# Streaming the moving operand's columns in other orders, in seven of twelve groups of a feed-forward block

## The chip, the cores and the metric

The kernel runs on one core of a Trainium2 chip. The metric is the device time of one execution in microseconds (us). Three runs of the kernel before gave 462.64, 462.67 and 462.92 us; the median is 462.67 us. The execution that the profiler recorded took 462.61 us.

The engines are named as the profile names them: PE is TensorE's matmuls, PEld its weight loads, DVE is VectorE, ACT is ScalarE, POOL is GpSimd, SP is SyncE with its DMA queue. A matmul here has a stationary operand (loaded first, 128 columns) and a moving operand, whose columns are streamed through; its output has one column for each column of the moving operand and lies in PSUM, where further matmuls add to it.

## The reference

Two stages follow each other. The first is a gated recurrence over 768 time steps for 4 batches and 8 heads of 40 channels; its outcome is a matrix x of 3072 tokens by 320 channels. The second is a feed-forward block on x:

```
h = x @ w_in                                       # 320 -> 2048
g = np.maximum(h, 0.0) + alpha * np.minimum(h, 0.0)
return (g @ w_out).astype(np.float32)              # 2048 -> 320
```

All of it is float32. The change touches the two matrix products of the second stage alone.

## The kernel before

The 3072 tokens are taken in 12 groups of 256 (`g` from 0 to 11), each of two chunks of 128. The recurrence is computed chunk by chunk as attention-like products, and the feed-forward of earlier groups is laid between those. The order of all work is written by hand: a list of named steps for the start (`ORDER`, line 638) and a pattern that repeats for each group (`PATTERN`, line 655). Each engine runs its instructions in that order.

Float32 accuracy is had by splitting each operand into a high part and a low part of type fp32r (`WH`, `WL`, `XH`, `XL`, `OH`, `OL`, `gh`, `gl`) and adding the products high by high, high by low and low by high.

The feed-forward of one group has 8 pairs of 128 hidden channels (`fp` from 0 to 7).

- Up (`up_steps`, line 703): for each of the two halves `e` of a pair, eight matmuls (lines 713 to 720) add to 256 columns of the PSUM tile `ph`. The stationary operand is a 128x128 block of the input weights, the moving operand is x by channel, one column for each of the group's 256 tokens. That is 16 matmuls for a pair and 128 for a group. ACT then takes the negative part (line 723), DVE adds the two slopes (line 728), ACT and POOL split the outcome into `gh` and `gl` (lines 737 and 739).
- Down (`down`, line 743; the matmul is line 750): the stationary operand is a 128x128 block of `gh` or `gl`, the moving operand is a row block of the output weights, `OH` or `OL`, of 320 columns. For each half `e` and each chunk `j` there are three matmuls, which add to `po[j]`. That is 12 for a pair and 96 for a group. The two PSUM tiles `po` have one buffer each: the next group's first down matmul needs the last copy out of them.
- Finish (`finish`, line 778): DVE copies the two `po` to `ob` in SBUF (line 783), and one DMA writes the group's 256 rows of the output (line 784).

Every matmul has its own weight load, which runs while the matmul before it streams.

Of the kernel before, what the change touches and what calls it, by code (L numbers as in the profile page):

```python
# [17 lines left out]
def kernel(ctx: ExitStack, tc: tile.TileContext, q, k, v, i_gate, f_gate, o_gate, w_in, w_out, alpha, out):  # L18
    nc = tc.nc
    B, H, S, D = q.shape  # L20
    DM, DFF = w_in.shape
    P = 128
# [30 lines left out]
    WH, WL = [None, None], [None, None]  # L53
# [5 lines left out]
    W2 = const.tile([P, DFF], F32R, tag="W2", name="W2")  # L59

    NB = 4
# [562 lines left out]
        yield  # L624

    NP = NF // 2
    LAG = 2
    LEAD = 4
    OFF = 0
# [6 lines left out]
    OBA = range(0)  # L636
# [54 lines left out]
    class FeedForward:  # L691
# [11 lines left out]
        def up_steps(self, split=True):  # L703
            g, fp = self.g, self.named
            self.named += 1
            XH, XL, X2, X2L = self.x
            ph = ps_h.tile([P, 2, GT], F32, tag="h", name=f"ph{g}_{fp}")
            for e in range(2):
                fs = slice((2 * fp + e) * P, (2 * fp + e + 1) * P)
                half, f0 = divmod((2 * fp + e) * P, DH)  # L710
                hs = slice(f0, f0 + P)
                dst = ph[:, e]
                nc.tensor.matmul(dst, WH[half][:, 0, hs], XH[:, 0], start=True, stop=False)  # L713
                nc.tensor.matmul(dst, WH[half][:, 1, hs], XH[:, 1], start=False, stop=False)  # L714
                nc.tensor.matmul(dst, WL[half][:, 0, hs], XH[:, 0], start=False, stop=False)  # L715
                nc.tensor.matmul(dst, WL[half][:, 1, hs], XH[:, 1], start=False, stop=False)  # L716
                nc.tensor.matmul(dst, W2[:, fs], X2, start=False, stop=False)  # L717
                nc.tensor.matmul(dst, WH[half][:, 0, hs], XL[:, 0], start=False, stop=False)  # L718
                nc.tensor.matmul(dst, WH[half][:, 1, hs], XL[:, 1], start=False, stop=False)  # L719
                nc.tensor.matmul(dst, W2[:, fs], X2L, start=False, stop=True)  # L720
            yield
            gt = late_pool.tile([P, 2, GT], F32, tag="g", name=f"g{g}_{fp}", bufs=3)
            nc.scalar.activation(gt, ph, AF.Relu, scale=-1.0)  # L723
            yield
            y = ph if split else gt
            for e in range(2):
                f = 2 * fp + e
                nc.vector.scalar_tensor_tensor(  # L728
                    out=y[:, e], in0=gt[:, e], scalar=oma[:, f : f + 1], in1=ph[:, e], op0=ALU.mult, op1=ALU.add
                )  # L730
            yield
            if g == 1 and fp < BEHIND:
                both = sb.tile([P, 2, 2, GT], F32R, tag=f"sp{fp % 2}", name=f"gg{g}_{fp}", bufs=1)
                gh, gl = both[:, 0], both[:, 1]
            else:
                gh, gl = (late_pool.tile([P, 2, GT], F32R, tag=f"g{x}", name=f"g{x}{g}_{fp}", bufs=3) for x in "hl")
            nc.scalar.copy(gh, y)  # L737
            yield
            (nc.vector if split else nc.gpsimd).tensor_tensor(gl, y, gh.bitcast(F32), ALU.subtract)  # L739
            self.done.append((gh, gl))  # L740
            yield

        def down(self, fp):
            if fp == 0 and self.g != 1:
                self.po = [ps_o.tile([P, DM], F32, tag=f"o{j}", name=f"po{self.g}_{j}") for j in range(GC)]
            po, (gh, gl) = self.po, self.done[fp]

            def add(e, j, x, W, **ends):
                f = 2 * fp + e
                nc.tensor.matmul(po[j], x[:, e, j * P : (j + 1) * P], W[f // NB][:, f % NB], **ends)  # L750

            def high(e, j):
                add(e, j, gh, OH, start=fp + e == 0, stop=False)
                add(e, j, gh, OL, start=False, stop=False)

            def low(e, j):
                add(e, j, gl, OH, start=False, stop=2 * fp + e == NF - 1)

            if self.g == NG - 1 and fp == NP - 1:

                for j in range(GC):
                    for step in (high, low):
                        for e in range(2):
                            step(e, j)
                    self.leave(j)
                return
            for step in (high, low):
                for e in range(2):
                    for j in range(GC):
                        step(e, j)  # L770
# [7 lines left out]
        def finish(self):  # L778
            g = self.g
            if g < NG - 1:  # L780
                ob = late_pool.tile([P, GC, DM], F32, tag="ob", name=f"ob{g}", bufs=1)
                for j in range(GC):
                    (nc.scalar.copy if g in OBA else nc.vector.tensor_copy)(ob[:, j], self.po[j])
                nc.sync.dma_start(out[g * GT : (g + 1) * GT, :].rearrange("(j p) e -> p j e", p=P), ob)
            if g == 1:
                turns[:] = ["b", "a"]
# [81 lines left out]
    def load_w_rest(i):  # L868

        pieces = []  # L870
        for e in range(2):
            cs = slice((i + e) * CW, (i + e + 1) * CW)
            rows, other = (slice(x * KR, (x + 1) * KR) for x in (e, 1 - e))
            pieces.append((rows, w_in[2 * P :, cs], W2[rows, cs], W2[other, cs]))
        return Weights(f"wr{i}", staging(f"wr{i}", ROOM[i][2]), pieces)

    def load_w_out(f):

        raw = sb.tile([P, 2, DM, 2], U32, tag="qS", name=f"wo{f}")
        src = w_out[f * P : (f + 2) * P, :].rearrange("(f p) c -> p f c", p=P)  # L880
        if src.dtype != F32:
            nc.sync.dma_start(
                raw.rearrange("p f c w -> p f (c w)"),
                w_out[f * P : (f + 2) * P, :].bitcast(U32).rearrange("(f p) c -> p f c", p=P),
            )
        to = slice(f % NB, f % NB + 2)

        def part(X):

            if X[f // NB] is None:  # L890
                out_block(f // NB)
            return lambda: X[f // NB][:, to]

        return Weights(f"wo{f}", raw, [(slice(0, P), src, lambda: part(OH)(), lambda: part(OL)())], False)
# [25 lines left out]
    def first_group():  # L920
# [333 lines left out]
        def block(name, make):  # L1254

            steps[name + "d"] = lambda: w.__setitem__(name, make())
            for op, do in dict(
                s=lambda: w[name].scale(), x=lambda: w[name].three(), y=lambda: w[name].shift(), j=lambda: w[name].join(),
                h=lambda: w[name].high(), H=lambda: w[name].high(1), l=lambda: w[name].low(), L=lambda: w[name].low(1),
                k=lambda: w[name].high(0, nc.gpsimd), K=lambda: w[name].high(1, nc.gpsimd),  # L1260
                p=lambda: w[name].low(0, nc.gpsimd), P=lambda: w[name].low(1, nc.gpsimd),
            ).items():
                steps[name + op] = do
# [4 lines left out]
        for i4 in (0, 2):  # L1268
            block(f"r{i4}", lambda i4=i4: load_w_rest(i4))
        for fp in range(NP):  # L1270
            block(f"o{fp}", lambda fp=fp: load_w_out(2 * fp))

        def named_ffn(g):
# [5 lines left out]
            steps[f"Z{g}"] = lambda: ffs[g].finish()  # L1279
            for fp in range(NP):  # L1280
                for tokens, split in (("URSGK", True), ("VrsgN", False)):
# [25 lines left out]
    start = len(nc.cur_bb.bb.instructions)  # L1307
# [34 lines left out]
```

## Time and profile before

| | |
|---|---|
| median of three runs | 462.67 us |
| the profiled execution, its own time | 462.61 us |
| its span (first to last instruction) | 460.9 us |
| PE busy | 454.9 us, 99% of the span |
| PEld busy | 444.1 us, 96% |
| DVE, ACT, POOL busy | 310.1, 314.0, 308.6 us |
| down matmuls in the program | 1152 of 320 columns |
| up matmuls in the program | 1536 of 256 columns |

Read it so: the engine that is busy all the time is PE, but a busy PE is not yet a PE at its peak, since matmuls are pipelined and their shown durations overlap. The time that one matmul takes of the span is the distance from its start to the start of the next one, not its shown duration (a down matmul is shown with some 308 ns, and the next one starts some 147 ns later). The rows below are mostly of that kind.

### The profile page before, as it was taken

How to read it: one execution, taken by the hardware profiler on the slowest of the kernel's cores; microseconds unless marked ns; L12 is line 12 of the kernel's file. 1: busy time of each engine (PE TensorE's matmuls, PEld its weight loads, DVE VectorE, ACT ScalarE, POOL GpSimd, SP SyncE). 2: the span in 40 equal slices, each digit the busy share in tenths (PEclk: the TensorE clock that was granted, in tenths of full speed). 3: DMA queues.
4: the chain of work that ended last, by engine and by line, in shares of the span. 5: the costliest groups of instructions: out<-in, count | busy, mean ns of one | idle time of the engine just before them, and what ended most of it. 6: DMA issues, size and time to landing. Idle time of an engine off the chain costs nothing.

```text
span 460.9 us, 11823 instructions
## 1 busy us (share of the span) xinstructions
PE 454.9 (99%) x4434; PEld 444.1 (96%) x4434; DVE 310.1 (67%) x659; ACT 314.0 (68%) x714; POOL 308.6 (67%) x398
## 2 busy tenths in 40 slices
PE   8999999999999999999999999999999999999997
PEld 6889999999999999999999999999999999999996
DVE  4789999667767766766676775776676675663321
ACT  4799898868858758758758659658758658423331
POOL 7735656756879679479779689479789687324231
PEclk9999999999999999999999999999999999999999
DMA  9997897749694673696793673598582341000000
GB/s 190 234 250 180 237 258 217 132 129 192 156 139 111 142 172 92 126 197 157 129 178 99 126 179 101 118 182 172 135 152 99 97 125 54 1 28 1 30 2 28
DMA packets 156163, 61.61 MB, mean 134 GB/s; under 512 B 140154, under 2 KB 145834, under 8 KB 156106
## 3 DMA queue, kind: packets, MB, share of 16 engines
q1 hardware_dynamic: 156026, 60.75, 58.8%
q8 instruction: 35, 0.57, 0.5%
q14 instruction: 22, 0.18, 0.2%
q10 hardware_dynamic: 80, 0.11, 0.1%
HBM read 36.90 MB, written 4.03 MB: 89 GB/s over the span
## 4 chain that ended last, share of the span: by engine, by line
PE 90%; DVE 4%; ACT 2%; SPq 2%; DMA 1%; issue 1%; DVEq 0%; ACTq 0%
PE po L750 36%; PE ph L713 5%; PE ph L716 5%; PE ph L718 5%; PE ph L715 5%; PE ph L714 5%; PE ph L717 5%; PE ph L720 5%; PE ph L719 5%; PE pH L376 4%; PE pS L477 4%; PE pH L337 1%; PE p L566 1%; PE pu L181 1%; PE pI L401 1%; PE pS L1071 1%
## 5 line engine op out<-in xcount | busy, mean ns | idle before, releaser
L739 POOL TENSOR_TENSOR gl<-g,gh 128x512 fp32r<-128x512 f32 x74 | 95.9, 1297 | 37.2 <-ACT gh L737 30.5
L750 PE MATMUL po<-OH,gh 128*128 128x320 f32 x368 | 110.2, 310 | 0.0
L750 PE MATMUL po<-OL,gh 128*128 128x320 f32 x368 | 109.4, 308 | 0.0
L723 ACT ACTIVATE g<-ph 128x512 f32<-128x512 f32 x96 | 57.5, 599 | 68.1 <-PE ph L720 62.6
L728 DVE SCALAR_TENSOR_TENSOR g<-g,oma,ph 128x256 f32<-128x256 f32 x148 | 63.5, 471 | 36.7 <-ACT g L723 36.7
L750 PEld LDWEIGHTS po<-OL,gh 128*128 128x128 f32 x368 | 69.2, 188 | 0.0
L750 PE MATMUL po<-OH,gl 128*128 128x320 f32 x368 | 69.0, 308 | 0.1
L750 PEld LDWEIGHTS po<-OH,gh 128*128 128x128 f32 x368 | 69.0, 187 | 0.0
L750 PEld LDWEIGHTS po<-OH,gl 128*128 128x128 f32 x368 | 57.7, 187 | 0.3 <-DVE gl L739 0.3
L713 PE MATMUL ph<-XH,WH 128*128 128x256 f32 x192 | 57.4, 299 | 0.5 <-DVE g L728 0.5
L716 PE MATMUL ph<-XH,WL 128*128 128x256 f32 x192 | 53.5, 279 | 0.0
L715 PE MATMUL ph<-XH,WL 128*128 128x256 f32 x192 | 53.4, 278 | 0.0
L714 PE MATMUL ph<-XH,WH 128*128 128x256 f32 x192 | 53.4, 278 | 0.0
L717 PE MATMUL ph<-X,W 128*128 128x256 f32 x192 | 53.3, 278 | 0.0
L718 PE MATMUL ph<-XL,WH 128*128 128x256 f32 x192 | 53.3, 278 | 0.0
L720 PE MATMUL ph<-X2L,W 128*128 128x256 f32 x192 | 53.3, 277 | 0.0
L719 PE MATMUL ph<-XL,WH 128*128 128x256 f32 x192 | 53.2, 277 | 0.0
L363 ACT CAST E<-pS 128x512 bf16<-128x512 f32 x72 | 41.1, 581 | 15.1 <-DVE pS L360 14.5
L448 ACT ACTIVATE E<-Lb,gates 128x128 f32<-128x128 f32 x160 | 50.1, 393 | 0.0
L737 ACT CAST gh<-g 128x512 fp32r<-128x512 f32 x74 | 44.7, 617 | 7.4 <-DVE g L728 5.0
L360 DVE TENSOR_TENSOR pS<-pS,E 128x512 f32<-128x512 f32 x36 | 24.9, 695 | 31.4 <-PE pS L477 28.9
L451 POOL TENSOR_SCALAR_AFFINE_SELECT E<-E 128x512 f32<-128x512 f32 x40 | 26.8, 670 | 20.0 <-ACT E L448 19.9
(196 smaller groups left out, 1138.3 us busy)
## 6 DMA issues: line engine op xcount, KB each, us to landing
Lb<-L_d SPq DMA_DIRECT2D x20, 512.0 KB
wo<-in_moe_w_out_dram SPq DMA_DIRECT2D x8, 640.0 KB
wi<-in_moe_w_in_dram SPq DMA_DIRECT2D x8, 512.0 KB
qn<-in_q_dram SPq DMA_DIRECT2D x24, 160.0 KB
kn<-in_k_dram SPq DMA_DIRECT2D x24, 160.0 KB
og<-in_o_gate_dram SPq DMA_DIRECT2D x24, 160.0 KB
va<-in_v_dram SPq DMA_DIRECT2D x24, 160.0 KB
out_dram<-ob SPq DMA_DIRECT2D x11, 320.0 KB
```

Source lines behind the costliest of these rows:

```text
L713: nc.tensor.matmul(dst, WH[half][:, 0, hs], XH[:, 0], start=True, stop=False)
L714: nc.tensor.matmul(dst, WH[half][:, 1, hs], XH[:, 1], start=False, stop=False)
L715: nc.tensor.matmul(dst, WL[half][:, 0, hs], XH[:, 0], start=False, stop=False)
L716: nc.tensor.matmul(dst, WL[half][:, 1, hs], XH[:, 1], start=False, stop=False)
L717: nc.tensor.matmul(dst, W2[:, fs], X2, start=False, stop=False)
L718: nc.tensor.matmul(dst, WH[half][:, 0, hs], XL[:, 0], start=False, stop=False)
L719: nc.tensor.matmul(dst, WH[half][:, 1, hs], XL[:, 1], start=False, stop=False)
L720: nc.tensor.matmul(dst, W2[:, fs], X2L, start=False, stop=True)
L723: nc.scalar.activation(gt, ph, AF.Relu, scale=-1.0)
L728: nc.vector.scalar_tensor_tensor(out=y[:, e], in0=gt[:, e], scalar=oma[:, f : f + 1], in1=ph[:, e], op0=ALU.mult, op1=ALU.add)
L739: (nc.vector if split else nc.gpsimd).tensor_tensor(gl, y, gh.bitcast(F32), ALU.subtract)
L750: nc.tensor.matmul(po[j], x[:, e, j * P : (j + 1) * P], W[f // NB][:, f % NB], **ends)
```

## The change

A row of 320 columns is 20 lines of 16 columns (64 bytes each), one of 256 columns is 16 lines. Two small functions rearrange an operand: `lines(x, a)` makes a view in which first every a-th line is taken, beginning with line 0, then every a-th line beginning with line 1, and so on. With a = 10 on 20 lines the order is 0, 10, 1, 11, 2, 12 and so on; with a = 4 it is 0, 4, 8, 12, 16, 1, 5 and so on. `in_order` cuts a row into the same pieces but leaves it in sequence.

- Down, groups 3 to 6, with a = 10, 4, 5 and 2: the moving operand (`OH`, `OL`) is streamed in the new order. `po` is written without gaps, so its columns stand in the order of the stream. The copy in `finish` puts them back: it reads `po` in sequence and writes `ob` line by line to their places.
- Up, groups 7 to 9, with a = 8, 4 and 2: the moving operand (x) and the output `ph` are both rearranged, so each sum lands in its place at once, and nothing behind it changes.
- In the other groups the value is None, and operands and outputs are as before. The up matmuls' eight lines became a loop with the same order of matmuls.

```diff
+    D_LINES = {3: 10, 4: 4, 5: 5, 6: 2}
+    U_LINES = {7: 8, 8: 4, 9: 2}
+
+    def lines(x, a):
+        return x if a is None else x.rearrange("p (h l c) -> p l h c", l=a, c=16)
+
+    def in_order(x, a):
+        return x if a is None else x.rearrange("p (l h c) -> p l h c", l=a, c=16)
...
-                nc.tensor.matmul(dst, W2[:, fs], X2L, start=False, stop=True)
+                pairs = [(W[half][:, kt, hs], X[:, kt]) for W, X in ((WH, XH), (WL, XH), (WH, XL)) for kt in range(2)]
+                pairs = pairs[:4] + [(W2[:, fs], X2)] + pairs[4:] + [(W2[:, fs], X2L)]
+                for i, (W, X) in enumerate(pairs):
+                    nc.tensor.matmul(
+                        lines(dst, U_LINES.get(g)), W, lines(X, U_LINES.get(g)), start=i == 0, stop=i == 7
+                    )
...
-                nc.tensor.matmul(po[j], x[:, e, j * P : (j + 1) * P], W[f // NB][:, f % NB], **ends)
+                row = lines(W[f // NB][:, f % NB], D_LINES.get(self.g))
+                nc.tensor.matmul(po[j], x[:, e, j * P : (j + 1) * P], row, **ends)
...
-                    (nc.scalar.copy if g in OBA else nc.vector.tensor_copy)(ob[:, j], self.po[j])
+                    nc.vector.tensor_copy(lines(ob[:, j], D_LINES.get(g)), in_order(self.po[j], D_LINES.get(g)))
```

No instruction moves on any engine: matmuls, copies and DMAs stand in the same order in both programs, at the same addresses. What differs in the rows are the shapes, and a few waits. On PE, where group 4's down matmuls begin (`po4` is that group's sums, `gh4_0` its first pair's high part), there stood before:

```order
L376 MATMUL pH11_1_3195<-vb11_2654,E3_11_2953 128x42
L750 MATMUL po4_0_3208<-OH0_104,gh4_0_3081 128x320
L750 MATMUL po4_0_3208<-OL0_105,gh4_0_3081 128x320
L750 MATMUL po4_1_3209<-OH0_104,gh4_0_3081 128x320
L750 MATMUL po4_1_3209<-OL0_105,gh4_0_3081 128x320
```

and now:

```order
L376 MATMUL pH11_1_3195<-vb11_2654,E3_11_2953 128x42
L758 MATMUL po4_0_3208<-OH0_104,gh4_0_3081 128x320 [waits PE_49]
L758 MATMUL po4_0_3208<-OL0_105,gh4_0_3081 128x320
L758 MATMUL po4_1_3209<-OH0_104,gh4_0_3081 128x320 [waits PE_49]
L758 MATMUL po4_1_3209<-OL0_105,gh4_0_3081 128x320
```

Two matmuls got a wait on PE's own semaphore, for the count that group 3's last down matmuls reach; the same is found at the start of groups 5, 6 and 7. In exchange, PE has 143 instructions that only wait, where it had 153.

On PE, the first half of group 7's first up block (`ph7_0`) was

```order
L713 MATMUL ph7_0_4775<-XH7_4650,WH0_102 128x256
L714 MATMUL ph7_0_4775<-XH7_4650,WH0_102 128x256
L715 MATMUL ph7_0_4775<-XH7_4650,WL0_103 128x256
L716 MATMUL ph7_0_4775<-XH7_4650,WL0_103 128x256
L717 MATMUL ph7_0_4775<-X27_4652,W2_76 128x256
L718 MATMUL ph7_0_4775<-XL7_4651,WH0_102 128x256
L719 MATMUL ph7_0_4775<-XL7_4651,WH0_102 128x256
L720 MATMUL ph7_0_4775<-X2L7_4653,W2_76 128x256
```

and is now

```order
L725 MATMUL ph7_0_4775<-XH7_4650,WH0_102 128x8x2x16 x2
L725 MATMUL ph7_0_4775<-XH7_4650,WL0_103 128x8x2x16 x2
L725 MATMUL ph7_0_4775<-X27_4652,W2_76 128x8x2x16
L725 MATMUL ph7_0_4775<-XL7_4651,WH0_102 128x8x2x16 x2
L725 MATMUL ph7_0_4775<-X2L7_4653,W2_76 128x8x2x16
```

The eight matmuls are the same ones in the same order, and only the shape of the output (and of the moving operand) differs.

## Rows read from the trace of the kernel before

**Rows 1.** The page's first part: busy time, share of the span and instructions of each engine; and from its second part the granted TensorE clock in 40 slices of the span, in tenths of full speed.

```profile
PE 454.9 (99%) x4434; PEld 444.1 (96%) x4434; DVE 310.1 (67%) x659; ACT 314.0 (68%) x714; POOL 308.6 (67%) x398
...
PEclk9999999999999999999999999999999999999999
```

**Rows 2.** Busy time of each engine in four stretches of the span; the columns are the stretch, its length, busy us and instructions of each engine, granted clock, DMA share and GB/s. Groups 3 to 9 have their changed work in the third.

```profile
0.00:20.00 20.00, 18.09 (x138) 14.19 (x139) 11.05 (x22) 12.65 (x32) 15.05 (x35) 1.00 0.96 196
20.00:113.00 93.00, 92.13 (x838) 89.05 (x837) 78.31 (x156) 79.51 (x174) 53.30 (x63) 1.00 0.85 206
113.00:393.00 280.00, 280.00 (x2927) 276.53 (x2924) 193.40 (x421) 200.02 (x470) 220.54 (x283) 1.00 0.62 134
393.00:461.00 68.00, 64.64 (x543) 64.30 (x540) 27.30 (x62) 21.84 (x40) 19.73 (x18) 1.00 0.04 16
```

**Rows 3.** What PE waited for, over the whole span: us in total, times, longest.

```profile
PE warm L154 <- POOL ident masks.py:199: 1.4, 1, 1.4
PE ph L713 <- DVE g L728: 0.5, 1, 0.5
PE pg L1161 <- DVE gates L979: 0.5, 1, 0.5
PE pb L1030 <- DVE E L1075: 0.3, 1, 0.3
```

**Rows 4.** The chain that ended last, its part from 148 to 393 us: shares by line.

```profile
by line: PE po L750 40.4%; PE ph L713 6.3%; PE pH L376 5.5%; PE ph L716 5.3%; PE ph L715 5.3%; PE ph L714 5.3%; PE ph L717 5.3%; PE ph L720 5.2%; PE ph L718 5.2%; PE ph L719 5.2%; PE pS L477 5.2%; PE pI L401 2.2%; PE p L566 1.9%; PE pu L181
```

**Rows 5.** The same chain's longest pieces of down matmuls: start us, us, what, and how many.

```profile
177.10 5.27 PE po L750 x36
...
212.23 5.27 PE po L750 x36
...
247.02 5.28 PE po L750 x36
...
281.92 5.28 PE po L750 x36
```

**Rows 6.** PE in order of time, an up block and a down block behind it: start us, us shown, line, operation, tiles, shape.

```profile
205.08 0.28 PE L713 MATMUL ph<-XH,WH 128*128 128x256 f32 x1
205.19 0.28 PE L714 MATMUL ph<-XH,WH 128*128 128x256 f32 x1
...
205.87 0.28 PE L720 MATMUL ph<-X2L,W 128*128 128x256 f32 x1
205.99 0.31 PE L750 MATMUL po<-OH,gh 128*128 128x320 f32 x1
```

**Rows 7.** The same view, another up block of the same shape (16 matmuls, of which the second and the last are shown, and what follows).

```profile
183.77 0.28 PE L714 MATMUL ph<-XH,WH 128*128 128x256 f32 x1
...
185.42 0.28 PE L720 MATMUL ph<-X2L,W 128*128 128x256 f32 x1
185.54 0.73 PE L477 MATMUL pS<-qS,kS 120*128 120x128 bf16 x10
```

**Rows 8.** The same view, two places near the start: a bf16 matmul whose moving operand is 128 columns read four times over (line 94), with the start of the next matmul; and six fp32 matmuls of 128 columns, each with its own fp32 weight load (line 566).

```profile
24.56 0.38 PE L94 MATMUL pb<-later,ident 128*128 128x512 bf16 x1
24.78 0.39 PE L1030 MATMUL pb<-LP,pick 96*128 96x128 bf16 x4
...
209.58 0.82 PE L566 MATMUL p<-ident,xn 128*128 128x128 f32 x6
```

**Rows 9.** The copies of a group's sums: all 14 between 148 and 393 us (duration min/median/max ns, first and last start), and who waited for them; then group 3's two, and PE where group 4's down matmuls begin.

```profile
L783 DVE COPY ob<-po x14: 480/486/492, 158.9 to 368.9; 128x320 f32<-128x320 f32 x14
...
who waited for it (us, times):
...
L783 DVE COPY ob<-po x2: 480/486/492, 193.7 to 194.2; 128x320 f32<-128x320 f32 x2
...
196.89 0.39 PE L750 MATMUL po<-OH,gh 128*128 128x320 f32 x1
```

**Rows 10.** PE waited for by others, between 148 and 393 us, at the up matmuls' tile: us in total, times.

```profile
who waited for it (us, times):
  ACT g L723: 32.0, 28
```

More of the change, by code (lines that the diff above doesn't have):

```diff
@@ L712, in up_steps @@
                 dst = ph[:, e]
[L713 to L719, printed above, removed]
-                nc.tensor.matmul(dst, W2[:, fs], X2L, start=False, stop=True)
+                pairs = [(W[half][:, kt, hs], X[:, kt]) for W, X in ((WH, XH), (WL, XH), (WH, XL)) for kt in range(2)]
[4 more added lines that the diff above has]
+                    )
             yield
```

## The prediction

> **What bounds the kernel now.** I read the busy shares first. [...] The stretches say where that holds without a gap: from 113 to 393 us PE is busy for 280.00 of 280.00 us [rows 2], and that stretch holds nearly all of the changed work. Third, what PE waited for: four waits, 2.7 us together, none on a copy or a transfer of the groups that change [rows 3]. Last the chain that ended last: between 148 and 393 us the down matmuls (line 750) have 40.4% of it, the eight up lines 5.2 to 6.3% each [rows 4]. So the reader is to see one thing: in the changed groups each nanosecond more or less between two matmul starts is a nanosecond of the span. Nothing else of the change lies on that path.
>
> **What one matmul takes.** A down matmul: 36 in a row take 5.27 or 5.28 us of the chain, 146.5 ns each [rows 5]. An up matmul: in one block starts go from 205.08 to 205.99 us over eight, 114 ns each (113.3 over longer stretches) [rows 6]; in another block, same shape, same clock, 15 steps from 183.77 to 185.54 us are 118 ns each [rows 7]. So up matmuls have two speeds. The mean over both: lines 714 to 720 have 5.2 to 5.3% of 245 us for 112 matmuls each, 114 to 116 ns [rows 4]; I take 115.
>
> **The change part by part.** Down, groups 3 to 6: 4 x 96 = 384 matmuls, 384 x 146.5 ns = 56.3 us of the span. Up, groups 7 to 9: 3 x 128 = 384 matmuls, 384 x 115 ns = 44.2 us. Neither their number, nor their columns, nor their order or addresses change; only the order of the 16-column lines within one stream does. A down matmul has 20 runs of 16 columns where it had one of 320, an up matmul 16 where it had one of 256: 384 x 20 + 384 x 16 = 13,824 runs.
>
> What a run costs, the trace of before does not show for fp32r. The nearest row is the bf16 matmul that reads 128 columns four times over, so that its stream jumps back three times: it takes 0.22 us for 512 columns, 0.43 ns a column, where the clock allows 0.417 [rows 8]. Its jumps cost at most some 3 ns each, and within the rounding nothing. But bf16 has half the bytes of fp32r in a column, so this row does not exclude a cost at full width. Bounds, then.
>
> Above: one TensorE cycle lost at each run. [...]
>
> [...] 320 columns at one per cycle are 133 ns, and a down matmul takes 146.5; if an order removed all of the difference, 384 x 13 ns = 5.1 us would go. [...]
>
> I take zero between -7.4 and +5.8. The down spacing is the same 146.5 ns in each long row of 36 [rows 5], although these rows take different weight blocks and have other engines and DMAs beside them; a cost that depended on which addresses meet would rather vary. And the jump row lies near zero.
>
> The copies: group 3 to 6 have two each, eight in all, 486 ns now [rows 9]; their output is now written in runs of 16 columns. Nobody waits for them. Group 3's end at 194.2 + 0.49 = 194.7 us, and PE first writes the tile again at 196.89 [rows 9]. Even at double the duration they would end at 195.7. DVE is busy for 193 of 280 us [rows 2], so 8 x 0.49 us more are no load. Zero.
>
> The waits: eight first down matmuls (two in each of groups 4 to 7) wait for PE's own count of the group before. That count is reached before the copy starts, at 193.7 us, and the waiting matmul starts at 196.89 [rows 9], 3 us later. Queued behind it would be all of PE, but it is met on arrival: zero. The ten instructions fewer that only waited stood beside streaming matmuls; zero too.
>
> The sum: 462.61 us of the profiled execution (460.9 us of span and 1.7 around it) + 0. The median of the runs is 462.67, 0.06 above, and I predict **462.7 us**.
>
> [...] The new up outputs are not contiguous, in pieces of 64 bytes. [...]
>
> **The rivals.**
>
> [...]
>
> *Faster: the extra 13 ns of a down matmul come from two reads that meet.* While 320 columns stream, the next 128 weight columns are read too; if both come to the same part of the memory from time to time, the order decides how often. For it: the extra itself, and the two speeds of up blocks that are alike in everything but the moment at which they start [rows 6, 7]: something falls into step or does not. Against it: the constancy over addresses. Some orders would then gain and some lose. If two of the four down orders reach 133 ns, 2 x 96 x 13 = 2.5 us go, and with the up groups always at 113.3, another 384 x 1.7 ns = 0.65: 459.5 us. [...]
> [...]
>
> *Slower: outputs written in pieces.* If the up output in pieces goes in at half speed, an up matmul takes 2 x 107 = 213 ns instead of 115, and 384 x 98 ns = 38 us are added: 500 us. ACT, which waits for the up matmuls 28 times already [rows 10], would only wait more. [...]
>
> That the change does nothing at all to the stream, because the hardware walks the same lines at the same pace, is the forecast itself.
>
> **How the numbers follow.** What the measurement can tell from no change is about 0.2%, 0.9 us, so "same" is 461.7 to 463.6. No measurable change 0.44; each run costs 0.24; outputs in pieces 0.06; faster 0.26. That gives faster 0.26, same 0.44, slower 0.30. The range: 457.5 leaves out the lower part of the faster case (some 0.05); 470 leaves out the pieces (0.06) and runs that cost over 1.3 cycles (some 0.08). The likeliest case's own range is 461.7 to 463.6.
>
> **What would show it.** Right: in groups 3 to 6, rows of 36 down matmuls at 5.27 us, in groups 7 to 9 up starts 113 to 118 ns apart, PE without waits, copies of any duration that nobody waits for. Wrong: a spacing in one changed group that differs from its unchanged neighbours (groups 2, 10, 11), and by how much for each value of a. A cost per run would be the same for a = 10, 4, 5 and 2, since all have 20 runs; a meeting of reads would differ between them. A wait of PE on itself at the start of groups 4 to 7, or a first matmul there later than after the copy, would say that the waits cost something after all.

## The result, and the profile after

The kernel with the change takes 466.21 us (median of three runs, 466.12 to 467.0) where the one before took 462.67: a ratio of 1.008, with a 95% interval of 1.0057 to 1.0103. It is slower by 3.5 us, 0.8%. The execution that the profiler recorded took 466.12 us, its span is 464.4 us, and 3.5 us more than before stand in both.

The page after, to be read beside [rows 1]: busy time of each engine, granted clock.

```profile
PE 458.2 (99%) x4434; PEld 447.4 (96%) x4434; DVE 311.2 (67%) x659; ACT 314.1 (68%) x714; POOL 308.3 (66%) x398
...
PEclk9999999999999999999999999999999999999999
```

PE has grown by 3.3 us at the same number of instructions and the same clock. DVE grew by 1.1, but not in the rearranged copies, which last as long as before (below); ACT and POOL stand still. So PE did not wait longer: it worked longer. The stretches say the same, answering to the last two of [rows 2] (stretch, its length, busy us and instructions of each engine, clock, DMA share, GB/s; the border is set 4 us later, where the program has come about as far).

```profile
113.00:397.00 284.00, 284.00 (x2940) 280.43 (x2938) 194.55 (x422) 200.18 (x471) 220.25 (x283) 1.00 0.61 132
397.00:465.00 68.00, 64.16 (x534) 63.82 (x532) 26.97 (x61) 21.84 (x40) 19.74 (x18) 1.00 0.04 16
```

PE is busy for 284.00 of 284.00 us. What PE waited for (us in total, times, longest; answers to [rows 3]):

```profile
PE warm L154 <- POOL ident masks.py:199: 1.4, 1, 1.4
PE pg L1169 <- DVE gates L987: 0.7, 1, 0.7
PE ph L725 <- DVE g L735: 0.5, 1, 0.5
PE pb L1038 <- DVE E L1083: 0.3, 1, 0.3
```

There is no new wait, and no row of PE waiting for itself or for a copy. So the 3.5 us lie in the distances between matmul starts, and the next view has them: PE at the tile `po` in groups 2 to 7, one group a row (stretch, length, busy us of these 96 matmuls, clock, DMA share, GB/s).

```profile
127.10:159.30 32.20, 14.95 (x96) 1.00 0.68 134
162.20:194.60 32.40, 15.41 (x96) 1.00 0.64 130
197.50:229.50 32.00, 15.17 (x96) 1.00 0.84 163
232.50:264.80 32.30, 14.98 (x96) 1.00 0.63 134
267.70:300.40 32.70, 15.47 (x96) 1.00 0.55 129
303.40:335.80 32.40, 14.97 (x96) 1.00 0.84 163
```

The first and the last row are groups left as they were. Between them stand a = 10, 4, 5 and 2: +0.46, +0.22, +0.03 and +0.52 us, 1.2 us in sum. The same for the up matmuls at the tile `ph`, groups 6 to 10; groups 7 to 9 have a = 8, 4 and 2:

```profile
254.30:283.20 28.90, 16.31 (x128) 1.00 0.66 150
289.70:319.20 29.50, 16.86 (x128) 1.00 0.83 156
325.20:354.60 29.40, 16.79 (x128) 1.00 0.65 147
360.90:390.20 29.30, 17.04 (x128) 1.00 0.38 108
396.60:423.70 27.10, 16.30 (x128) 1.00 0.04 13
```

Beside the two unchanged groups that is some +0.6, +0.5 and +0.7 us. A busy time counts overlapping matmuls once, so it is only near the distance of starts; start to start over all matmuls of the trace, the up matmuls take 2.3 us more than before (2.0 of them in groups 7 to 9, and 0.2 in group 1, which is unchanged), the down matmuls 1.3, and all others together none.

The chain shows the distance itself, in the pieces of 36 down matmuls that answer to [rows 5]: start us, us, what, how many.

```profile
177.52 5.44 PE po L758 x36
...
212.96 5.37 PE po L758 x36
...
247.90 5.28 PE po L758 x36
...
283.13 5.41 PE po L758 x36
...
319.17 5.28 PE po L758 x36
```

Divided by 36: 151.1 ns in group 3, 149.2 in 4, 146.7 in 5, 150.3 in 6, and 146.7 in group 7, which is as before. From here on a spacing is the mean distance from a matmul's start to the next one's, within the blocks of one group; the few first steps of a block that are 80 to 110 ns longer than the rest are left out. In the whole trace it is 146.5 in unchanged down groups and 151.2, 148.8, 146.8 and 151.7 for a = 10, 4, 5 and 2; in unchanged up groups 114 to 116.5, and 120.0, 119.8 and 121.4 for a = 8, 4 and 2.

The copies, answering to [rows 9]:

```profile
L791 DVE COPY ob<-po x14: 480/486/492, 159.1 to 371.8; 128x320 f32<-128x320 f32 x14
...
who waited for it (us, times):
```

To write the columns back in pieces of 16 costs a copy nothing, and still nobody waits for it.

### The profile page after: what moved, and what is told of

It is laid out like the page before. It is cut to its first block, busy times and chain, and to the rows that moved or that the text cites. A ratio compares the mean times of both kernels' runs of the same rounds, so it can differ in the third digit from the quotient of the medians.

```text
span 464.4 us, 11813 instructions
## 1 busy us (share of the span) xinstructions
PE 458.2 (99%) x4434; PEld 447.4 (96%) x4434; DVE 311.2 (67%) x659; ACT 314.1 (68%) x714; POOL 308.3 (66%) x398
## 4 chain that ended last, share of the span: by engine, by line
PE 92%; DVE 4%; ACT 2%; issue 1%; POOL 0%; POOLq 0%; DVEq 0%; ACTq 0%
PE ph L725 38%; PE po L758 36%; PE pH L376 4%; PE pS L477 4%; PE warm L154 2%; PE pH L337 1%; PE p L566 1%; PE pu L181 1%; PE pI L401 1%; PE pS L1079 1%; PE pqk L261 1%; PE pb L1025 1%; PE pI L395 1%; DVE t_wo L841 0%; DVE OL L853 0%
## 5 line engine op out<-in xcount | busy, mean ns | idle before, releaser
L725 PE MATMUL ph<-XH,WH 128*128 128x256 f32 x384 | 80.1, 290 | 0.5 <-DVE g L735 0.5
L725 PE MATMUL ph<-XH,WL 128*128 128x256 f32 x384 | 76.2, 280 | 0.0
L725 PE MATMUL ph<-XL,WH 128*128 128x256 f32 x384 | 76.0, 279 | 0.0
L725 PEld LDWEIGHTS ph<-XH,WH 128*128 128x128 f32 x384 | 59.3, 189 | 1.1 <-ACT gh L744 0.6
L725 PEld LDWEIGHTS ph<-XL,WH 128*128 128x128 f32 x384 | 58.5, 188 | 0.2 <-DVE XL L585 0.2
L725 PEld LDWEIGHTS ph<-XH,WL 128*128 128x128 f32 x384 | 58.7, 189 | 0.0
```

The source lines that it names most:

```text
L725: nc.tensor.matmul(lines(dst, U_LINES.get(g)), W, lines(X, U_LINES.get(g)), start=i == 0, stop=i == 7)
```

## The experiments

The question is what in the new order costs a matmul its 0 to 5 ns. The theories at the start are those of the prediction: each run of 16 columns costs a little; the moving operand's reads meet those of the next weights; the output in pieces costs (up only). To them comes one that the result suggests: the order of the moving operand's lines has a speed of its own ("own steps"), whatever else is read. All edits are shown against the changed kernel. One run of the kernel before on the same chip took 461.99 us beside the first four.

**Up: input and output apart.** The moving operand alone is rearranged in some groups, the output alone in others, both in group 9. Where only one is, the columns of `ph` don't stand in their places.

```diff
-    U_LINES = {7: 8, 8: 4, 9: 2}
+    U_X = {3: 8, 5: 4, 7: 2, 9: 8}
+    U_OUT = {4: 8, 6: 4, 8: 2, 9: 8}
...
-                        lines(dst, U_LINES.get(g)), W, lines(X, U_LINES.get(g)), start=i == 0, stop=i == 7
+                        lines(dst, U_OUT.get(g)), W, lines(X, U_X.get(g)), start=i == 0, stop=i == 7
```

(The table of the down groups is empty here.)

> Down is as in the kernel before in all groups. Up: groups 3, 5 and 7 rearrange only the moving operand (a = 8, 4, 2), groups 4, 6 and 8 only the output (a = 8, 4, 2), group 9 both (a = 8); so the columns of h stand in other places than the reference's in groups 3 to 8. Unchanged up matmuls are 115 ns apart. Theory 'reads' (the order in which the moving lines are read decides): 120, 120 and 121 ns in groups 3, 5 and 7, 115 in groups 4, 6 and 8, 120 in group 9. Theory 'pieces' (the output in pieces decides): 115 in groups 3, 5, 7 and 120 to 121 in groups 4, 6, 8.

Measured 464.7 us, 2.7 above the kernel before. PE at `ph` in groups 3 to 6, as above:

```profile
148.10:177.20 29.10, 16.85 (x128) 1.00 0.64 146
183.60:212.40 28.80, 16.24 (x128) 1.00 0.78 158
218.30:247.70 29.40, 16.79 (x128) 1.00 0.68 148
254.10:282.60 28.50, 16.30 (x128) 1.00 0.67 152
```

The rows alternate. Groups 3 and 5, with the moving operand rearranged, have 16.85 and 16.79, the values that the change gave to the same a; with group 7 the spacings are 120.0, 119.8 and 121.4 ns. Groups 4 and 6, with the output alone in pieces, have 16.24 and 16.30, as unchanged ones; with group 8 the spacings are 115.0, 115.5 and 114.8. Group 9 with both has 120.0, as group 3 with the input alone. So the cost is all in the order of what is read, and pieces of 64 bytes in the output are free.

**Down: single steps.** The moving operand is replaced by reads that isolate a step from one line of 16 columns to the next; the sums are then others than the reference's.

```diff
+    MOVING = {
+        2: lambda x: again(x, 5, 64), 3: lambda x: stepped(x, 20, 2), 4: lambda x: stepped(x, 20, 3),
+        5: lambda x: stepped(x, 20, 4), 6: lambda x: again(x, 20, 16), 7: lambda x: again(x, 10, 32),
+        8: lambda x: again(x, 2, 160), 9: lambda x: x[:, :320].rearrange("p (h l c) -> p l h c", l=2, c=80),
+    }
...
-                nc.tensor.matmul(po[j], x[:, e, j * P : (j + 1) * P], row, **ends)
+                nc.tensor.matmul(po[j], weights_of(x, e, j, self.g), moving(W, f, self.g), **ends)
```

Here `again(x, n, c)` reads the first c columns n times, and `stepped(x, 20, s)` reads 20 lines, each s lines behind the last; `weights_of` gives the ordinary weights in this run.

> Up is as before in all groups. The down matmuls of eight groups read other weight columns than the reference asks for, still 320 of them in pieces of 16-column lines, and their output is not put back: group 2 one piece of 64 columns five times, group 3 every second line, group 4 every third, group 5 every fourth, group 6 one line twenty times, group 7 a piece of 32 columns ten times, group 8 a piece of 160 columns twice, group 9 four pieces of 80 columns in the order 0, 2, 1, 3. Theory 'own steps' (a step of one line, counted modulo four, is free, other steps cost, whatever the weight load does): 146.5 ns in groups 2, 8 and 9 (within 1), 152 in group 3 (as a = 2), 151 in group 4, 149 in groups 5 and 6 (as a = 4), 149 in group 7. Theory 'meeting' (the moving reads meet the reads of the next weights): groups 5 and 6, which stay in one of four parts of the memory while the weights pass through all, are met for about a quarter of the time only: no more than 146.5, and alternating from matmul to matmul. A fixed cost per run: 146.5 in groups 2, 8 and 9, and the same number, whichever it is, in groups 3 to 6.

Measured 463.88 us. PE at `po`, groups 2, 3, 5, 6, 7 and 9:

```profile
126.40:158.60 32.20, 14.95 (x96) 1.00 0.67 134
161.60:193.90 32.30, 15.34 (x96) 1.00 0.62 131
...
231.80:264.50 32.70, 15.24 (x96) 1.00 0.59 132
267.40:299.70 32.30, 15.24 (x96) 1.00 0.57 131
302.60:334.60 32.00, 15.12 (x96) 1.00 0.88 165
...
372.90:404.80 31.90, 14.98 (x96) 1.00 0.19 54
```

Five times 64 columns, twice 160, and four pieces of 80 in another order cost nothing (146.5 to 146.7 ns): a jump as such is free. Every second, third and fourth line: 150.5, 149.9 and 149.3 ns. One line read 20 times, with no distance at all: 149.4, the same as every fourth. Ten times 32 columns, where half of the steps are in sequence: 148.2, about half the extra. The theory of own steps had all of these within 1.5 ns; "meeting" had 146.5 or less in groups 5 and 6, and missed. By these rows alone a fixed cost of some 0.17 ns a run (an estimate: 3.4 ns over 20 runs) would come near most of them too. That "each run costs" is out by the change: a = 10, 4, 5 and 2 all have 20 runs, and their costs are 4.7, 2.3, 0.3 and 5.2 ns. So it is the step that counts. A step of one line is free, and so, in the change, was a step of five (a = 5, 146.8); steps of 0, 2, 3 and 4 lines cost 3 to 4 ns over 20 of them.

**The weights' place.** If reads meet, the place of the weight columns that are loaded meanwhile must matter. The moving operand is in sequence; the stationary one is a single column read 128 times (groups 2, 3 and 6), every second or fourth column (4 and 5), or a block shifted by 1, 2 or 3 lines (7 to 9).

```diff
+    WEIGHTS = {
+        2: lambda x: one(x, 0), 3: lambda x: one(x, 1), 4: lambda x: sparse(x, 2), 5: lambda x: sparse(x, 4),
+        6: lambda x: one(x, 2), 7: lambda x: x[:, 16:144], 8: lambda x: x[:, 32:160], 9: lambda x: x[:, 48:176],
+    }
```

> The moving operand and up are as before in all groups; the down matmuls of eight groups load other weights than the reference asks for: groups 2, 3 and 6 one column 128 times over (from the first, second and third 64-byte line), group 4 every second column, group 5 every fourth, groups 7, 8 and 9 128 columns in sequence that begin one, two and three lines later. Theory 'own steps': the weights do not matter, 146.5 ns (within 1) in all groups. Theory 'meeting': weights of one line are read once or always in one part of the memory; groups 2, 3 and 6 fall to 134 to 141 ns, group 5, which touches four times as many lines, rises to 150 or more, and groups 7 to 9 may differ from 146.5 in either direction.

Measured 471.38 us. PE at `po`, groups 2, 4, 5 and 7:

```profile
126.90:159.10 32.20, 14.98 (x96) 1.00 0.68 134
...
196.80:229.00 32.20, 15.23 (x96) 1.00 0.78 164
231.90:272.70 40.80, 23.44 (x96) 1.00 0.52 106
...
310.50:342.30 31.80, 14.95 (x96) 1.00 0.86 166
```

Weights from one place only, or shifted by a line or more, leave 146.3 to 146.7 ns. Weights from every fourth column raise the spacing to 233 ns, and 8.5 us of this kernel's 9.4 are that one group (23.44 against 14.95): there the load itself, 128 columns 16 bytes apart, is longer than the stream, as the weight loads of that group show (count, shown ns min/median/max, first and last start, shape):

```profile
L782 PEld LDWEIGHTS po<-OH,gl x24: 329/329/329, 236.6 to 267.4; 128*128 128x128 f32 x24
```

They are shown with 329 ns where ordinary ones, those of the up matmuls beside them, are shown with 0.19 us. Every second column costs 149.3. A load can thus be slow by its own stride, but with the moving operand in sequence nothing here hints that it disturbs the stream by its place.

**Moving lines against weight lines.** The sharper form: the moving operand reads every fourth line (groups 2 to 5) or every second (6 to 9), the weights are one column, from line 1, 2, 3 and 4 in turn.

```diff
+    MOVING = {
+        **{g: lambda x: stepped(x, 20, 4) for g in (2, 3, 4, 5)}, **{g: lambda x: stepped(x, 20, 2) for g in (6, 7, 8, 9)},
+    }
+    WEIGHTS = {g: lambda x, o=(g - 2) % 4: one(x, o) for g in range(2, 10)}
```

> Up is as before. The down matmuls of groups 2 to 5 read every fourth line of the moving operand, those of groups 6 to 9 every second; their weights are one column 128 times over, from the first line in groups 2 and 6, the second in 3 and 7, the third in 4 and 8, the fourth in 5 and 9 (other weights and other columns than the reference asks for). Theory 'own steps': 149 ns in groups 2 to 5, 152 in groups 6 to 9, whichever line the weights are in. Theory 'meeting': in groups 2 to 5 the two reads are in the same part of the memory for one line of the four alone: one group at 155 ns or more, the other three at 134 to 140; in groups 6 to 9 two and two.

Measured 467.78 us, and spacings of 153.0, 151.6, 153.0 and 152.9 ns, then 151.3, 151.4, 151.3 and 151.3. No place stands out as the theory had it (one group at 155 or more beside three at 134 to 140), so the meeting of the two reads by their place is refuted in this form too. One thing stays unexplained: the level is 1 to 4 ns above the same steps with ordinary weights (149.3 and 150.5), although these loads are shown with 188 ns, as ordinary ones are. With a stepped moving operand the weights do bear on the spacing, and how is open.

**The two parts by themselves**, each timed in three rounds. Down alone has the table of the change for `po` and none for `ph`; up alone the reverse.

```diff
-    D_LINES = {3: 10, 4: 4, 5: 5, 6: 2}
+    D_LINES = {3: (10, 16), 4: (4, 16), 5: (5, 16), 6: (2, 16)}
...
-    U_LINES = {7: 8, 8: 4, 9: 2}
+    U_LINES = {}
```

(A value is now the pair of a and the columns in a piece; 16 is the piece of the change.)

> The change's down orders alone, up as before. By the spacings of the changed kernel's trace (96 x 4.7 + 96 x 2.3 + 96 x 0.3 + 96 x 5.2 ns): 1.2 us slower than before, and the spacings 151, 149, 147 and 152 ns in groups 3 to 6 again. If the down copies or the waits of PE on itself cost something too, more than that.

> The change's up orders alone, down as before. By the spacings of the changed kernel's trace (128 x 4.7 + 128 x 4.7 + 128 x 6.5 ns): 2.0 us slower than before; 120, 120 and 121 ns in groups 7 to 9. The two halves together then make 3.2 of the change's 3.5 us; if they add to clearly less, something that only both together do is left to find.

Down alone: 463.89 us against 462.70, ratio 1.0027 (1.0016 to 1.0038), +1.2 us. Up alone: 465.05 us, ratio 1.0049 (1.0032 to 1.0066), +2.35 us. Their sum is 3.54 us, and so is what the change took: the parts add. Each has an interval of its own (0.5 us to either side for down, 0.8 for up), so a term for copies, waits or a coupling of the two is not excluded below about 1 us, but nothing points to one. The groups that were changed have the spacings of the change (151.2, 148.8, 146.8 and 152.5, where the last was 151.7; 120.0, 119.8 and 121.4 ns).

**Smaller pieces.** Is the old order the best, and is the unit 64 bytes? Every pair below is a true order: copies and outputs put the columns back.

```diff
+    D_LINES = {2: (2, 4), 3: (4, 4), 4: (5, 4), 5: (8, 4), 6: (10, 4), 7: (16, 4), 8: (20, 4), 9: (40, 4)}
+    U_LINES = {2: (2, 64), 3: (4, 32), 4: (2, 32), 5: (16, 8), 6: (2, 8), 7: (32, 4), 8: (2, 4), 9: (4, 4)}
...
+        return x if ac is None else x.rearrange("p (h l c) -> p l h c", l=ac[0], c=ac[1])
```

> True reorderings, every sum put back. Down: pieces of 4 columns (16 bytes) with a = 2, 4, 5, 8, 10, 16, 20, 40 in groups 2 to 9. Up: group 2 pieces of 64 columns with a = 2, group 3 pieces of 32 with a = 4, group 4 of 32 with a = 2, group 5 of 8 with a = 16, group 6 of 8 with a = 2, group 7 of 4 with a = 32, group 8 of 4 with a = 2, group 9 of 4 with a = 4. Theory 'own steps, four parts of 64 bytes': up 115 ns in group 2 (each step is one line, counted modulo four), 117 to 118 in groups 3 and 4 (every second step is another). With pieces of 16 bytes it says no more than that a piece which shares its 64 bytes with no neighbour costs more than one that does: if the chip fetches 64 bytes at a time, all eight down groups are at 200 ns or more; if it fetches 16 bytes at a time, they stay under 160 and differ by a, with the least for a = 5 (a step of 5 pieces, one modulo four). Theory 'any order other than the row's own costs': all eight up groups at 118 or more.

Measured 472.51 us, beside 462.70 for the kernel before. The chain's pieces of 36 in groups 2, 3, 4 and 7, pieces of 16 bytes (4 columns), a = 2, 4, 5 and 16:

```profile
142.41 5.28 PE po L758 x36
...
177.58 5.09 PE po L758 x36
...
213.77 6.00 PE po L758 x36
...
324.97 6.07 PE po L758 x36
```

The second row is the surprise: 5.09 us, 141.4 ns each (141.8 in the group's mean). An order of 16-byte pieces, every fourth one first, is *faster* than the sequence. With the step counted in 16-byte pieces, and modulo 16, the spacings are: 1 146.5; 2 146.4; 4 142 to 144 (a = 4 and 20); 8 153 to 155 (a = 8 and 40); 10 153.4; 5 166.5; 0 (a = 16) 168.9. My own guess had made a = 5 the fastest, and it is the second slowest; none of the eight is at 200 ns, and two are above 160, so neither size of a fetch that I had named fits. That every order but the sequence costs is refuted as well. Up, pieces of 256 bytes are free (115.3 ns), those of 128 bytes cost as those of 64 (118.8 and 120.0), and the rest reach from 114.3 (a = 4, 16 bytes) to 127.0. So in up, too, every fourth 16-byte piece costs nothing: the same group had 114.8 in the kernel before.

**The rest of 13 ns.** A down matmul takes 146.5 ns where its 320 columns at 0.417 ns are 133.3; the 0.417 is an estimate from the spacings of 336 and 384 columns below, 20.0 ns for 48 columns at a granted clock of 1.00. Does the rest belong to each matmul or to each column? Groups 2 to 9 stream 336 to 512 columns, in sequence, into a wider `po`.

```diff
+    WIDE = {2: 336, 3: 352, 4: 384, 5: 416, 6: 448, 7: 480, 8: 512, 9: 512}
...
+                nc.tensor.matmul(self.wide[j][:, :w] if w > DM else po[j], x[:, e, j * P : (j + 1) * P], row, **ends)
```

> Up as before; the down matmuls of groups 2 to 9 stream 336, 352, 384, 416, 448, 480, 512 and 512 columns in sequence from the start of the weight tile (other columns than the reference asks for, and more). It measures where the 13 ns above one column per cycle come from. If fp32r streams slower by itself: 0.45 ns a column, 175 ns at 384 and 233 at 512. If the next weight load takes 13 ns once from each matmul: 146.5 ns and 0.417 for each further column, 173 at 384 and 226.5 at 512.

Measured 500.94 us, beside the same 462.70; spacings 153.4, 160.1, 173.4, 188.6, 200.1, 218.1 and 230.7 ns (the last for 512 columns). Less 0.417 a column, 13.4, 13.4, 13.4, 15.3, 13.4, 18.1 and 17.4 ns remain: up to 384 columns it is one sum for each matmul, at 480 and 512 some 4 to 5 ns more. At 384 columns that is the expectation of once per matmul (173.4 against 173 and 175); at 512 it lies between the two, nearer to the slower stream (230.7 against 226.5 and 233; in the chain's pieces of 36 it is 8.40 us, 233.3 ns each). What the 13 ns are stays open.

**The fast order everywhere.** All 12 down groups read 16-byte pieces with a = 4; the up matmuls are as in the kernel before. The last group's copies (in `leave`, on ACT) put the columns back too.

```diff
+    D_LINES = {g: (4, 4) for g in range(12)}
+    U_LINES = {}
...
-            nc.scalar.copy(ob, self.po[j])
+            nc.scalar.copy(lines(ob, D_LINES.get(self.g)), in_order(self.po[j], D_LINES.get(self.g)))
```

> Every sum put back. All twelve groups' down matmuls stream pieces of 4 columns (16 bytes) with a = 4, the order that took 141.8 ns in one group; up as before. If that gain is the order's own: 1152 x 4.7 ns = 5.4 us faster than before, some 457.3 us where before is 462.7, and 142 ns in every group. If it was luck of one group's addresses or phase: spacings from 142 to 147 from group to group, and a gain between 0 and 5 us. If the copies in 16-byte pieces cost something on the way: less than the spacings say.

Five rounds: 459.65 us against 462.98, ratio 0.9935 (0.9921 to 0.9948). This beats both kernels, but by 3.3 us, not by the 5.4 expected. Two views say why. PE at `po`, one row of many alike; and PE at `ph`, groups 3 and 4, first in the kernel before and then in this one:

```profile
196.30:227.90 31.60, 14.51 (x96) 1.00 0.82 167
```

```profile
148.70:177.10 28.40, 16.21 (x128) 1.00 0.64 151
183.50:212.30 28.80, 16.21 (x128) 1.00 0.78 156
```

```profile
148.50:176.90 28.40, 16.38 (x128) 1.00 0.64 133
183.10:211.80 28.70, 16.39 (x128) 1.00 0.77 158
```

The down spacing is 142.0 in each group from 1 to 10, 14.51 us where it was 14.95; start to start the down matmuls gave 4.7 us. But the up matmuls, of which the edit changes no operand and no shape, went from 16.21 to 16.39 us a group. More of their steps are at the slower of the two speeds of [rows 6] and [rows 7]: in groups 3 to 9 it is 58% of them with 116 ns or more, where it was 35%. The mean is 116.2 ns where it was about 115, and 1.4 us went back that way. The matmuls outside the feed-forward took 0.3 more. The copies in 16-byte pieces last 480 to 492 ns, as before, so they are not what the gain lost.

**More orders, and the same kernel once more.** First a scan with pieces of 8, 16 and 32 bytes, to find a rule:

```diff
+    D_LINES = {2: (8, 2), 3: (20, 8), 4: (2, 8), 5: (10, 8), 6: (40, 2), 7: (4, 8), 8: (4, 2), 9: (20, 4)}
+    U_LINES = {2: (8, 2), 3: (4, 8), 4: (8, 4), 5: (16, 4), 6: (2, 2), 7: (16, 2), 8: (4, 2), 9: (8, 8)}
```

> True reorderings, every sum put back; pieces of c columns with a, down: group 2 c = 2, a = 8 (a step of 64 bytes), group 3 c = 8, a = 20 (640 bytes), group 4 c = 8, a = 2 (64), group 5 c = 8, a = 10 (320), group 6 c = 2, a = 40 (320), group 7 c = 8, a = 4 (128), group 8 c = 2, a = 4 (32), group 9 c = 4, a = 20 again (320). Up: group 2 c = 2, a = 8, group 3 c = 8, a = 4, group 4 c = 4, a = 8, group 5 c = 4, a = 16 (256 bytes), group 6 c = 2, a = 2, group 7 c = 2, a = 16, group 8 c = 2, a = 4, group 9 c = 8, a = 8 (256 bytes). Theory 'own steps, in 64 bytes modulo 256' (a step that moves each piece on by 64 bytes, modulo 256, is the best one): groups 2, 4, 5, 6 and 9 of down under 146.5 ns, groups 3 and 7 above 150, group 8 at 146.5. Up: groups 5 and 9 worst (125 or more). Theory 'that order alone': no other group under 146.

Measured 562.71 us, beside 462.98. The chain's pieces of 36 in groups 2, 3 and 7:

```profile
160.02 9.76 PE po L758 x36
202.95 5.35 PE po L758 x36
...
388.57 5.06 PE po L758 x36
```

Pieces of 8 bytes take 272, 276 and 290 ns in the three groups that have them, about twice the 133 of the columns alone (320 at 0.417). In 32-byte pieces a = 20, 2 and 10 take 148.6, 147.0 and 147.5, and a = 4 takes 142.5 (140 in most steps, 137 to 183 in the others). The theory of steps of 64 bytes had groups 2, 4, 5 and 6 below 146.5, groups 3 and 7 above 150, group 8 at 146.5 and group 9's up matmuls at 125 or more: all eight missed (the last with 117.7). Group 9's 143.9 down and group 5's 136.4 up came as it had them. The theory of that order alone had no other group under 146, and missed with groups 7 and 9. No rule that I formed holds for pieces under 64 bytes.

Then the two fastest orders on one chip, in five rounds: 32-byte pieces with a = 4 in all groups, and the 16-byte kernel of above again.

```diff
+    D_LINES = {g: (4, 8) for g in range(12)}
```

> Every sum put back. All twelve groups' down matmuls stream pieces of 8 columns (32 bytes) with a = 4, the order that was at 140 ns in step and at 142.5 over its one group. If the step locks in most blocks: 1152 x 4.5 to 6 ns = 5 to 7 us less, minus what the up matmuls give back as they did with pieces of 4 (some 1.5 us): 457.5 to 459.5 us. If up gives nothing back this time: 456 to 458. If the one group was luck: 460 to 463.

> The kernel of e9_best_down once more, beside the one with pieces of 8 on the same chip. By its first timing: 3.3 us faster than before, down 142 ns and up 116.2 in the groups from 3 to 9, as before with the kernel before at 146.5 and 115. If the loss of 1 ns in up was that run's alone, up is at 115 and the kernel some 4.8 us faster.

32-byte pieces: 460.91 us against 462.69, ratio 0.9962 (0.9948 to 0.9976); the spacing varies between the groups from 141.5 to 145.7. That time lies among those expected if the one group was luck, but it was not: each group is below the 146.5 of before, only less far than hoped, and the up matmuls gave back 1.5 us here too. 16-byte pieces: 459.21 us, ratio 0.9922 (0.9907 to 0.9936), with 142.0 ns down and 116.2 up again in groups 3 to 9. So the gain and the part of it that the up matmuls give back repeat.

## Where the prediction was right and where it was wrong, point by point

The forecast was 462.7 us, no change that could be measured, and the change took 466.2. That lies inside the stated range of 457.5 to 470, but only by luck: the upper part of the range came from a cost at each run, and that mechanism is refuted below.

- **What bounds the kernel: right.** PE is busy for 284.00 of 284.00 us, and the 3.5 us of the result are 2.3 + 1.3 us of distances between starts. What held for the frame held for the sum's other terms as well: the copies are as long as before and nobody waits for them, PE has no wait for itself at the start of groups 4 to 7, and the two parts alone add up to the whole. The zeros for the copies and the waits stand.
- **"I take zero between -7.4 and +5.8": the step that failed.** The cost of the new orders was +1.2 to 1.3 us down and +2.0 to 2.35 up. It lay inside the bounds, and the value taken was wrong. No run shows the bounds themselves: not a cycle lost at each run, on which the +5.8 stands, and of the -7.4 only the 5.1 us that are 384 times the 13 ns. What the runs showed in their place is 0.3 to 5.2 ns more for a down matmul of the change, 4.7 to 6.6 for an up matmul, and as a gain 4.5 ns for a down matmul in 16-byte pieces (146.5 to 142.0). Two reasons carried it. The constant 146.5 ns of [rows 5] says that the spacing doesn't depend on which weight block is streamed; but all these blocks are read in the *same* order, so the row says nothing on the order. And the bf16 row [rows 8] jumps back three times over 128 columns: three jumps in 512 columns, each after a long piece. The single steps showed that such jumps are free for fp32r too (five times 64 columns, 146.5). The 0.417 ns a column that the prediction sets beside the row, and with it the 133 and the 13 ns of a down matmul, are what the run with more columns shows: 20.0 ns for 48 further columns, and 13.4 ns beside the columns from 336 to 384. What the row doesn't hold is a step at every 16 columns. I had named its weakness as the width of the data, and it was as much the number and the kind of its steps. Between ends far apart I went to the row that was near in form, and it had none of what the change does.
- **"Each run costs" (0.24): the right sign, and the wrong mechanism.** It gives the same cost for every a. The change has 4.7, 2.3, 0.3 and 5.2 ns in down. An order with four times as many pieces (16 bytes, a = 2) stays at 146.4. The prediction's last paragraph had said that this comparison would decide, and it did, before any experiment. Nor does the number of runs order the costs of the two kinds: 4.7 to 6.6 ns for each up matmul, with 16 runs, and 0.3 to 5.2 for a down matmul, with 20.
- **"Two reads that meet": refuted as a conflict by place.** With the moving operand in sequence, neither weights read from one column nor weights shifted by lines change the spacing (146.3 to 146.7). Nor do the line classes stand out against each other as the rival needs (151.3 to 153.0). Not every coupling of the two reads is excluded: the same steps took 1 to 4 ns more with one-column weights than with ordinary ones. What the rival said beside it, that some orders would gain, holds for pieces smaller than 64 bytes: 142.0 ns.
- **"Outputs in pieces": refuted.** 115.0, 115.5 and 114.8 ns with the output alone in pieces. At half speed, as that rival has it, they would be at 213.

What is shown: the spacing of these matmuls depends on the order in which the moving operand is read, and the other things that the change altered (outputs in pieces, copies, waits) cost nothing that these runs can tell. Against the sequence, orders of 64-byte lines cost 0 to 6.6 ns a matmul, and orders of 16-byte pieces in down -5 to +22 ns. What is open: why a step of 1 or 5 lines is free and one of 0, 2, 3 or 4 is not, and so what in the hardware the order acts on; why the same a costs up and down matmuls differently (a = 4: 4.8 and 2.3 ns); why every fourth 16-byte piece is faster than the sequence; why up matmuls fall more often into their slower speed with other down matmuls between them. Other places of the moving operand in memory, and other types than fp32r, were not tried.

## What to carry to other kernels

Where PE is busy without a gap, the distance from start to start is the price list, and a row bounds an access pattern only if it has the same steps, not merely some jump; constancy over blocks that are read alike is no evidence about reading them otherwise. If an order is free to choose and the copy behind it can put the columns back at no cost, one kernel with another order in each group measures eight of them at once. A gain found so in one part must then be timed in the whole: here 4.7 us in the down matmuls became 3.3 in all.

## What was not expected of the hardware

- fp32r columns in sequence are not the fastest: 320 columns take 146.5 ns in sequence, 142.0 as every fourth 16-byte piece, 168.9 as every sixteenth, and 272 to 290 in 8-byte pieces. Orders of whole 64-byte lines lie from 146.8 to 151.7.
- Weights 16 bytes apart load so slowly that they set a pace of 233 ns; weights 8 bytes apart allow 149.3, and a single column read 128 times is as quick as a block while the moving operand is in sequence (146.3 to 146.7).
- In group 6 of the change the distances lock into alternating 146 and 154 ns for long stretches, where group 3 has 150 to 154 throughout.
- The 13 ns that a matmul takes beyond its columns are the same from 320 to 384 columns (13.2 to 13.4).
- The up matmuls' two speeds [rows 6, 7] follow something outside their own block: with other down orders between them, the same blocks went from about 115 to 116.2 ns in the mean, in two runs of that kernel alike.
